# Loading the last two keys of each partition of one K unit by 32 small transfers, in a cached-attention decode layer

## The chip, the cores and the metric

The kernel runs on one core of one Trainium2 chip. The metric is the device time of one execution in microseconds (us), lower is better. Before the change three runs gave 669.81, 669.94 and 670.23 us, a median of 669.94 us. The profile shown here was taken from a separate execution of 670.03 us, of which the span from the first to the last instruction is 668.3 us.

## The reference

One decode step (one new token for each of 4 sequences) of a transformer layer: a layer norm, attention over a cache of 4096 keys and values for each of 32 heads of width 128, an output projection with a residual, then a second layer norm and a small MLP with a Mish activation.

```python
def _A_ref(x, k_cache, v_cache, wq, wo):            # x: 4 x 1 x 640
    q = (x @ wq).reshape(B, Sq, H, Dh).transpose(0, 2, 1, 3)
    scores = jnp.einsum("bhqd,bhkd->bhqk", q, k_cache) * (Dh ** -0.5)
    p = _softmax(scores, axis=-1)
    o = jnp.einsum("bhqk,bhkd->bhqd", p, v_cache)
    return o.transpose(0, 2, 1, 3).reshape(B, Sq, H * Dh) @ wo
...
h = x + _A_ref(_layernorm(x), A_k_cache, A_v_cache, A_wq, A_wo)
h2 = h + _B_ref(_layernorm(h), B_w1, B_b1, B_w2)    # 640 -> 1728 -> 640
```

All tensors are bf16. The K cache and the V cache are 134 MB each (4 x 32 x 4096 x 128 numbers of 2 bytes), the weights some 15 MB together, and everything is read once.

## The kernel before, in words

**Units.** The caches are worked through in 16 units. A unit is 8 heads of one sequence: 8 x 4096 keys, laid on 128 partitions with 16 partitions to a head, so that a partition holds R = 256 consecutive keys of 128 numbers, 64 KB that also lie in one piece in HBM. A unit of K or of V is thus 8.39 MB. The names are `kt0` to `kt15` and `vt0` to `vt15`.

**Slots.** SBUF holds three slots of that size (L71, `bufs=3`), taken in turn: `first` (the query weights `wq` and small inputs), `kt0`, `kt1`, then `vt0` in the place of `first`, `kt2` in that of `kt0`, `vt1` in that of `kt1`, and so on. A load into a slot has to wait until what was there has been read. At the end two slots hold the weights of the projection and the MLP (`wend`, `wend2`).

**Transfers.** All large loads are issued by SyncE, SP for short, in program order: `wq` (L101), then `kt0` and `kt1` (L104 and L105, through `load_kv`, whose `dma_start` is L89), then `vt0` (L239), and in the main loop `kt(u+2)` (L373) and `vt(u+1)` (L378). Two small inputs, `x` (L100, 4 partitions) and `b1` (L102, 1 partition), are issued by ScalarE (ACT). SP is a single sequence: what is queued behind a waiting instruction waits as well. The transfers themselves run on 16 DMA engines.

**Landing signals.** Nobody writes semaphores by hand: the framework gives each transfer one of eight semaphores, in turn over all transfers in program order, ACT's and SP's alike. A reader waits on the semaphore of the transfer it needs. When a transfer gets a semaphore that an earlier one has had, its issue waits until that earlier one has landed. In the program's list of instructions the eight are called DMAHW0 to DMAHW7.

**Compute.** For each unit `scores(u)` multiplies the keys in place by the broadcast query on VectorE (DVE, L263, eight multiplications of 64 keys by 64 columns), sums them with matmuls against the identity (PE, L270) and reductions (DVE, L251). `softmax(u)` (L286 on) takes the maximum and the exponentials (ACT, L309). `pv(u-1)` multiplies with the values of the unit before (PE, L325), and `close` divides by the sums. After the loop come the projection and the MLP.

Of the kernel before, what the change touches and what calls it, by code (L numbers as in the profile page):

```python
# [16 lines left out]
def kernel(  # L17
# [13 lines left out]
    nc = tc.nc  # L31

    B, Sq, D = A_x.shape
    _, H, Sk, Dh = A_k_cache.shape
    F = B_w1.shape[1]
    N = B * Sq
    DC = D // 128
    G = 8
    PH = 128 // G
    R = Sk // PH  # L40
# [38 lines left out]
    def slot(name):  # L79
        return slots.tile([128, SLOT], BF16, tag="kv", name=name)  # L80

    def load_kv(kind, cache, u, parts=1):
        o, b = divmod(u, N)
        t = slot(f"{kind}{u}")
        tv = t[:, :].rearrange("p (r d) -> p r d", d=Dh)
        view = cache[b, G * o : G * (o + 1)].rearrange("h (p r) d -> (h p) r d", p=PH)
        for i in range(parts):
            r0, r1 = i * R // parts, (i + 1) * R // parts
            nc.sync.dma_start(out=tv[:, r0:r1, :], in_=view[:, r0:r1, :])  # L89
        return tv  # L90


    first = slot("first")
    wq_sb = first[:, 0 : DC * H * Dh].rearrange("p (c n) -> p c n", c=DC)
# [7 lines left out]
    nc.scalar.dma_start(out=b1_row, in_=B_b1.rearrange("(o f) -> o f", o=1))  # L102
    kts, vts = {}, {}
    kts[0] = load_kv("kt", A_k_cache, 0)  # L104
    kts[1] = load_kv("kt", A_k_cache, 1)  # L105


    ident = consts.tile([128, 128], BF16)
# [49 lines left out]
    for src, dst in ((ln1_v, xT), (x_v, xT_res)):  # L158
# [10 lines left out]
        out=own1[:, :], in_=ident[:, :].rearrange("p (i k) -> p i k", i=G), axis=AX.X, op=ALU.add  # L169
    )  # L170
    nc.vector.tensor_scalar(
        out=own[:, :], in0=own1[:, :], scalar1=-1.0, scalar2=1e30, op0=ALU.add, op1=ALU.mult
    )
    nc.vector.tensor_reduce(
        out=sel[:, :, :],
        in_=ident[:, :].rearrange("p (t i r) -> p r i t", t=CT, r=RQ),
# [5 lines left out]
        out=dq_f[:, :], in_=ident[:, :].rearrange("p (q j) -> p q j", j=J), axis=AX.X, op=ALU.add  # L182
# [4 lines left out]
        out=j_f[:, :], in_=ident[:, :].rearrange("p (q j) -> p j q", j=J), axis=AX.X, op=ALU.add  # L187
# [287 lines left out]
    for dst in (h2T, hc):  # L475
        nc.vector.tensor_tensor(
            out=dst,
# [10 lines left out]
    for c in range(FC):  # L488
# [9 lines left out]
        if c == 4:  # L498
# [3 lines left out]
                out=std, in_=v_ps[:, :], func=ACT.Sqrt, bias=eps_t[:, :], scale=1.0  # L502
# [4 lines left out]
    def fcn():  # L507
# [4 lines left out]
        out=h1n,  # L512
# [6 lines left out]
        out=h1s,  # L519
# [8 lines left out]
        out=tb, in0=ta, scalar=2.0, in1=ta, op0=ALU.add, op1=ALU.mult  # L528
# [3 lines left out]
        out=tc_, in0=tb, scalar1=-0.5, scalar2=-1.0, op0=ALU.mult, op1=ALU.add  # L532
# [5 lines left out]
        out=act_t, in0=td, scalar=1.0, in1=h1s, op0=ALU.add, op1=ALU.mult  # L538
# [5 lines left out]
    for i, (w2, c) in enumerate(w2_of):  # L544
        rows = 128 if c < C2 else FREM
# [10 lines left out]
        out=oT.rearrange("p n c -> p c n"), in0=hT, in1=y2T[:, :, :], op=ALU.add  # L556
# [43 lines left out]
```

## Time and profile before

| what | value |
|---|---|
| median of 3 runs | 669.94 us (669.81 to 670.23) |
| the profiled execution | 670.03 us, span 668.3 us |
| moved from HBM | 283.35 MB, 424 GB/s over the span |
| time of SP's packets, share of 16 DMA engines | 98.7% |
| PE busy | 383.0 us (57%) |
| DVE busy | 353.2 us (53%) |
| ACT busy | 86.8 us (13%) |

The page gives each engine's busy time and its share of the span; the span in 40 slices of 16.7 us with the busy tenths of each engine, and the rate of the DMA engines; the DMA queues; the chain of work that ended last; the costliest groups of instructions; and the DMA issues. The trace behind it can be asked for the instructions of a line or a tile, for waits, and for the DMA share in any stretch of time. A DMA share of 1.00 means that the 16 engines were busy all the time (packets are counted where they start, so a short stretch can show more than 1). SPq and ACTq are the instructions with which SP and ACT issue transfers. "Landing" is the moment at which a transfer's semaphore says that it is complete.

### The profile page before, as it was taken

To read this page: it belongs to the slowest core of one execution; us is meant where nothing else is said; L and a number is where in the kernel's file an instruction comes from. 1 tells how busy PE (TensorE), PEld (TensorE's weight loads), DVE (VectorE), ACT (ScalarE), POOL (GpSimd) and SP (SyncE) were. 2 spreads that over 40 slices of the span, in tenths; PEclk is the share of its full clock that TensorE was granted. 3 is DMA by queue.
4 is the path that set the end of the run, shared out by engine and by line. 5 is a ranking of instruction groups with operands and counts; after the bars stand their busy time and mean duration, and the time that the engine had idled before them with its cause. 6 is when DMAs were issued, how large, how long until landed. Compare 5 with 4: busy or idle time off the path is not lost.

```text
span 668.3 us, 6430 instructions
## 1 busy us (share of the span) xinstructions
PE 383.0 (57%) x2793; PEld 179.8 (27%) x2793; DVE 353.2 (53%) x314; ACT 86.8 (13%) x314; POOL 1.4 (0%) x10
## 2 busy tenths in 40 slices
PE   0366758375572738557283765738285573728754
PEld 0222323132231313223031322313132231313343
DVE  2078848183663818366381935738192664818321
ACT  0102020202011020202002020110202011020211
POOL 0000000000000000000000000000000000000000
PEclk9998979679696968969698886979888696977965
DMA  9999999999999999999999999999999999999996
GB/s 377 440 439 432 439 433 432 436 428 429 428 436 435 429 432 432 432 436 432 432 432 437 436 421 435 432 436 432 432 428 432 435 432 439 432 440 399 423 415 208
DMA packets 8293, 283.78 MB, mean 425 GB/s; under 512 B 771, under 2 KB 2503, under 8 KB 3144
## 3 DMA queue, kind: packets, MB, share of 16 engines
q1 hardware_dynamic: 8254, 283.35, 98.7%
q8 instruction: 22, 0.36, 0.2%
q14 instruction: 7, 0.06, 0.0%
q10 hardware_dynamic: 10, 0.01, 0.0%
HBM read 283.35 MB, written 0.01 MB: 424 GB/s over the span
## 4 chain that ended last, share of the span: by engine, by line
DMA 59%; DVE 25%; PE 12%; issue 2%; SPq 0%; DVEq 0%; ACT 0%
DMA kt<-in_A_k_cache_dram 55%; DVE kt L263 21%; PE s L270 6%; DMA wend<-in_B_w_dram 5%; PE o L325 4%; DVE s_sb L251 3%; DVE pm L289 1%; PE tr L291 0%; PE tr L302 0%; DVE mx L295 0%; PE h_ps L491 0%; PE y2T L547 0%; SPq L388 0%; DVE otn L354 0%; DVE rl L353 0%
## 5 line engine op out<-in xcount | busy, mean ns | idle before, releaser
L270 PE MATMUL s<-kt,ident 128*128 128x512 bf16 x1024 | 269.7, 418 | 223.6 <-DVE kt L263 223.6
L263 DVE TENSOR_TENSOR kt<-kt,qb 128x4096 bf16<-128x4096 bf16 x128 | 288.1, 2283 | 191.1 <-DMA kt<-in_A_k_cache_dram 191.1
L270 PEld LDWEIGHTS <-ident 128*128 128x128 bf16 x1024 | 108.6, 106 | 378.3 <-issue 148.4
L309 ACT ACTIVATE e<-s_sb,nb 128x256 bf16<-128x256 f32 x128 | 63.1, 494 | 219.0 <-DVE nb L304 219.0
L251 DVE TENSOR_REDUCE s_sb<-s 128x64 f32<-128x512 f32 x64 | 43.9, 687 | 54.6 <-PE s L270 32.6
L325 PE MATMUL o<-vt,e 128*32 128x512 bf16 x1024 | 66.2, 416 | 4.4 <-DMA vt<-in_A_v_cache_dram 4.4
L237 ACT CAST qb<-qb_ps 128x128 bf16<-128x128 f32 x16 | 4.2, 265 | 306.4 <-PE qb_ps L229 306.4
L325 PEld LDWEIGHTS <-e 128*32 128x32 bf16 x1024 | 28.1, 104 | 34.4 <-issue 13.7
L309 ACT ACTIVATION_READ_ACCUMULATOR e<-s_sb,nb 128x1 f32 x128 | 23.8, 186 | 0.0
L291 PE MATMUL tr<-ident_f,pm 128*1 128x128 f32 x32 | 6.1, 270 | 21.3 <-DVE pm L289 21.3
L344 PE MATMUL oT<-sel,o_sb 128*128 128x8 f32 x128 | 17.5, 263 | 1.1 <-ACT o_sb L333 1.1
L344 PEld LDWEIGHTS oT<-sel,o_sb 128*128 128x128 f32 x128 | 16.4, 201 | 1.3 <-ACT o_sb L333 1.3
L353 DVE RECIPROCAL rl<-oT 128x8 f32<-128x8 f32 x16 | 3.2, 199 | 17.0 <-PE oT L344 17.0
L333 ACT COPY o_sb<-o 128x512 f32<-128x512 f32 x16 | 9.1, 569 | 14.7 <-PE o L325 14.7
L202 PE MATMUL qT_ps<-xT,first 128*128 128x4 bf16 x160 | 4.4, 167 | 10.0 <-DMA first<-in_A_wq_dram 10.0
L302 PE MATMUL tr<-mx,nscale 1*128 1x8 f32 x32 | 6.1, 262 | 5.9 <-DVE mx L295 5.9
L291 PEld LDWEIGHTS tr<-ident_f,pm 128*1 128x1 f32 x32 | 1.8, 80 | 28.7 <-issue 28.7
L295 DVE TENSOR_REDUCE mx<-tr 1x8 f32<-1x128 f32 x16 | 4.5, 279 | 9.0 <-PE tr L291 9.0
L302 PEld LDWEIGHTS tr<-mx,nscale 1*128 1x128 f32 x32 | 4.7, 183 | 10.6 <-DVE mx L295 10.6
L216 DVE COPY b1T<-b_ps 128x13 f32<-128x13 f32 x1 | 0.2, 173 | 13.4 <-PE b_ps L213 13.4
L202 PEld LDWEIGHTS <-first 128*128 128x128 bf16 x160 | 4.3, 104 | 10.1 <-DMA first<-in_A_wq_dram 10.1
L340 PEld LDWEIGHTS oT<-rs,ones_f 128*128 128x128 f32 x32 | 6.1, 198 | 3.3 <-issue 1.3
(77 smaller groups left out, 71.8 us busy)
## 6 DMA issues: line engine op xcount, KB each, us to landing
vt<-in_A_v_cache_dram SPq DMA_DIRECT2D x4, 2048.0 KB, 44.0
first<-in_A_wq_dram SPq DMA_DIRECT2D x1, 5120.0 KB, 15.5
wend<-in_A_wo_dram SPq DMA_DIRECT2D x4, 1280.0 KB, 21.3
wend<-in_B_w_dram SPq DMA_DIRECT2D x1, 2160.0 KB
wend<-in_B_w_dram SPq DMA_DIRECT2D x3, 640.0 KB, 17.8
kt<-in_A_k_cache_dram SPq DMA_DIRECT2D x16, 47.9
vt<-in_A_v_cache_dram SPq DMA_DIRECT2D x15, 35.2
wend<-in_B_w_dram SPq DMA_DIRECT2D x1, 160.0 KB, 28.2
```

Source lines behind the costliest of these rows:

```text
L202: nc.tensor.matmul(qT_ps[:, h, :], lhsT=wq_sb[:, c, h * Dh : (h + 1) * Dh], rhs=xT[:, c, :], start=(c == 0), stop=(c == DC - 1),)
L251: nc.vector.tensor_reduce(out=s_sbs[u][:, part * RP : (part + 1) * RP], in_=s_ps[:, :, :], axis=AX.X, op=ALU.add,)
L263: nc.vector.tensor_tensor(out=kt[:, :, d0 : d0 + DQ], in0=kt[:, :, d0 : d0 + DQ], in1=qbs[u][:, d0 : d0 + DQ].unsqueeze(1).to_broadcast([1 ...
L270: nc.tensor.matmul(s_ps[:, :, :], lhsT=ident[:, :], rhs=kt[:, :, d : d + W], start=(d == 0), stop=(d == Dh - W),)
L289: nc.vector.tensor_reduce(out=pm[:, :], in_=s_sb[:, :], axis=AX.X, op=ALU.max)
L291: nc.tensor.matmul(tr_ps[0:1, 0:128], lhsT=pm[:, :], rhs=ident_f[:, :], start=True, stop=True)
L302: nc.tensor.matmul(nb_ps, lhsT=nscale[:, :], rhs=mx[:, :], start=True, stop=True)
L309: nc.scalar.activation(out=e2[:, :, i, :], in_=s_sb[:, :].rearrange("p (g r) -> p g r", r=RQ), func=ACT.Exp, bias=nb[:, i : i + 1], scale= ...
L325: nc.tensor.matmul(o_ps[t : t + G * RQ, :], lhsT=e2[:, g, :, :], rhs=vt[:, g * RQ : (g + 1) * RQ, :], start=(g < CT), stop=(g >= NGV - CT),)
L333: nc.scalar.copy(out=o_sb[:, :], in_=o_ps[:, :])
L340: nc.tensor.matmul(oT_ps[:, 1, :], lhsT=ones_f[:, :], rhs=rss.pop(u)[:, :], start=True, stop=True)
L344: nc.tensor.matmul(oT_ps[:, 0, :], lhsT=o_sb[:, r * Dh : (r + 1) * Dh], rhs=sel[:, r, :], start=(r == 0), stop=(r == RQ - 1),)
```

## The change

`kt1` is loaded by a new helper. One transfer brings the first 254 keys of all 128 partitions. The last two keys of each partition (512 bytes a partition, 64 KB in all) come by 32 transfers: 8 of 8 partitions (partitions 0 to 63), 8 of 4 partitions (64 to 95) and 16 of 2 partitions (96 to 127). All are issued by SP between the load of `kt0` and that of `vt0`. The data and all later work are the same.

```diff
+    def load_k_uneven(u, tail=2):
+
+        o, b = divmod(u, N)
+        t = slot(f"kt{u}")
+        tv = t[:, :].rearrange("p (r d) -> p r d", d=Dh)
+        view = A_k_cache[b, G * o : G * (o + 1)].rearrange("h (p r) d -> (h p) r d", p=PH)
+        nc.sync.dma_start(out=tv[:, 0 : R - tail, :], in_=view[:, 0 : R - tail, :])
+        for rows, lo, hi in ((8, 0, 64), (4, 64, 96), (2, 96, 128)):
+            for p in range(lo, hi, rows):
+                nc.sync.dma_start(
+                    out=tv[p : p + rows, R - tail : R, :], in_=view[p : p + rows, R - tail : R, :]
+                )
+        return tv
...
     kts[0] = load_kv("kt", A_k_cache, 0)
-    kts[1] = load_kv("kt", A_k_cache, 1)
+    kts[1] = load_k_uneven(1)
```

## The prediction

> **What bounds the kernel now.** I read the page first. The DMA row and the queue row say that the kernel is a stream of bytes:
>
> ```profile
> DMA  9999999999999999999999999999999999999996
> GB/s 377 440 439 432 439 433 432 436 428 429 428 436 435 429 432 432 432 436 432 432 432 437 436 421 435 432 436 432 432 428 432 435 432 439 432 440 399 423 415 208
> ...
> q1 hardware_dynamic: 8254, 283.35, 98.7%
> ```
>
> Every slice but the last is at nine tenths or more, while PE and DVE are busy for 57% and 53%. Then I asked for the DMA share by stretches (columns: stretch, its length, busy time of PE, PEld, DVE, ACT and POOL with counts, clock, DMA share, GB/s):
>
> ```profile
> 0.00:1.60 1.60, 0.00 (x0) 0.00 (x0) 0.21 (x2) 0.02 (x1) 0.94 (x8) 1.00 0.00 0
> ...
> 200.00:400.00 200.00, 114.74 (x739) 51.26 (x727) 107.10 (x85) 27.60 (x105) 0.00 (x0) 0.84 1.00 433
> 400.00:560.00 160.00, 91.45 (x572) 40.77 (x572) 85.68 (x68) 20.00 (x76) 0.00 (x0) 0.83 1.00 433
> ```
>
> From 36 to 560 us the share is 1.00 at 433 GB/s: there is no gap in which a lost microsecond could be made up. A unit of 8.39 MB takes 8.39 MB / 433 GB/s = 19.4 us. Whatever leaves the DMA engines without work is added to the end. The question is thus whether SP still queues `vt0` before `kt1` has gone through.
>
> SP's own timeline up to 60 us (start, duration, instruction) and the landings of `kt0` and `kt1`:
>
> ```profile
> 0.74 0.42 SPq L101 DMA_DIRECT2D first<-in_A_wq_dram  x1
> 1.22 0.89 SPq L89 DMA_DIRECT2D kt<-in_A_k_cache_dram  x2
> 21.30 0.33 SPq L89 DMA_DIRECT2D vt<-in_A_v_cache_dram  x1
> 58.52 0.33 SPq L89 DMA_DIRECT2D kt<-in_A_k_cache_dram  x1
> ```
> ```profile
> DMA to landing us min/median/max: 34.7/44.4/54.1
> ```
>
> `kt1` is the second of the pair, issued at 1.7 us, with the longest time: it lands at 1.7 + 54.1 = 55.8 us. `vt0` was queued at 21.3 us, 34 us ahead of need. That is the cover which the change touches.
>
> **What is added, and what it waits for.** One issue becomes 33. A semaphore that comes round again makes the issue wait, and the waits of SP show it in the tail (who waits, for whom, total us, times, longest):
>
> ```profile
> SPq L399 <- DMA wend<-in_A_wo_dram: 1.1, 1, 1.1
> ```
>
> L399 loads `w2` into a slot of its own; nothing in it needs `wo` (L388). It waits for `wo` only because it is given the same semaphore.
>
> Counted in program order: `x` has semaphore 0, `wq` 1, `b1` 2, `kt0` 3, the large part of `kt1` 4. The small transfers go on from there. Numbers 1 to 3 take 5, 6 and 7, which are fresh. Number 4 takes 0 again and waits for `x`, number 5 for `wq`, number 6 for `b1` (early), number 7 for `kt0`, and **number 8 takes semaphore 4 and waits for the large part of `kt1`**. The list of the changed program's instructions has these waits, DMAHW3 on the seventh and DMAHW4 on the eighth. Behind number 8 in SP's single sequence stand numbers 9 to 32 and then `vt0`. At 55.8 us nothing else is queued: the DMA engines run dry, and SP still has 25 small issues (8 to 32) to make before `vt0`.
>
> **Price of one small issue.** The trace of before has no issue of 8, 4 or 2 partitions on SP. Nearest rows by place: the four issues of `wo` take 1.75 us together, the two of `kt` 0.89 us, so 0.44 to 0.47 us each with the gap between them. These four at 624.4 us include one whose semaphore had come round and was free. By size, ACT's two small issues bound it:
>
> ```profile
> 0.73 0.55 ACTq L100 DMA_DIRECT2D first<-in_A_x_dram  x1
> 1.31 0.23 ACTq L102 DMA_DIRECT2D first<-in_B_b_dram  x1
> ```
>
> Four partitions took 0.55 us (0.58 to the next start), one partition 0.23 us, 0.27 with a gap of 0.04; SP's store of 20 partitions (L568) took 0.39. I take 0.47 us, SP's own spacing, which lies between, and keep 0.27 and 0.58 for the range. 25 x 0.47 = 11.8 us (6.8 to 14.5).
>
> That holds if a small transfer lands before its semaphore comes round eight issues later, 8 x 0.47 = 3.8 us. The store at the end is issued at 666.1 us and everything is over at 668.3; `x`, issued at 0.73 us, let DVE start at 3.19. Both are under 2.5 us, so the spacing decides and not the landing.
>
> **Sum.** `vt0` is issued at 55.8 + 11.8 = 67.6 us instead of 21.3. What does the stream lose? Restarting costs what it costs at the launch. Up to the end of `kt1` the engines move 5.24 (`wq`) + 8.39 + 8.39 = 22.02 MB, at 433 GB/s 50.9 us, after a start-up S counted from the span's beginning; so on the mean they finish at 50.9 + S. Restarted, they are as good as at full rate S - 0.74 after the issue (the issue of `wq` was at 0.74 us). The loss is 67.6 + (S - 0.74) - (50.9 + S) = 16.0 us, in which S cancels. The large part is 2 of 256 keys shorter: 0.15 us off, 15.8.
>
> That is the mean of 16 engines. With S = 2.2 us (the first slice moved 377 instead of 433 GB/s for 16.7 us: 2.2 us lost) they finish at 53.1 us, while the last landing is at 55.8: some engines run late. If an engine that is late here is also the one that ends the kernel, it loses less, for the pause lets it catch up: at most the 2 us or so between the two times, which gives 13.8. No view names the engines, so I keep both and take 15.5, nearer to the mean.
>
> In a sentence apart: the Trainium skill ("DMA: Bandwidth & Descriptors", section "Latency and other measured facts") gives about 600 ns to the first byte of a transfer issued by SP; here the first packets start between 1.60 and 1.80 us, some 1.0 us after the issue at 0.74. By the page's figure the sum would be 0.4 us lower, 15.1; the measurement decides.
>
> **What costs nothing.** The 64 KB themselves move while the engines are idle anyway. The multiplications of `kt1` start at 61.06 us as before, since only those of the last 64 keys need the small pieces; they come some 16 us later, and the last piece should land by 69 or 70. So `kt1` is used up as before and `vt1` is issued at 84.7 as before. `vt0` lands at 75.1 + 15.5 = 90.6 instead of 75.1 (21.3 + 53.8 in its row); the matmuls of `pv(0)`, at 87.1 before, wait until then, and `kt3`, queued behind them, is issued 3.5 us later, at 94.3, while `kt2` is still moving (88.5 to 110). No second gap, and after that everything is shifted alike.
>
> 670.03 + 15.5 = 685.5 us in the profiled execution; the median of before lies 0.09 us under it, so **685.4 us**.
>
> **Rivals.**
> 1. *Hidden: not slower.* If number 8 didn't have to wait for `kt1`, SP would go on from `kt0`'s landing (1.2 + 34.7 = 35.9 us), issue 26 pieces by 48.1 us and `vt0` right then, ahead of the 53 us at which the engines get free. That is the point from which it decides: `vt0` queued before 52. What is left is the pieces' own time: between -0.15 us (an engine relieved of its share of them) and +2.4 us (all 64 KB on one engine at 433 / 16 = 27 GB/s); with the pieces spread unevenly over some engines about +0.5, so 670.4 us. For it: `vt0` has 34 us of cover. Against it: the wait on DMAHW4 is in the program, and L399's row shows that such waits hold. Chance 0.05, within no change mostly.
>    The Trainium skill (same page, section "Issuing engines are not separate DMA queues") says that the sequencer's time to start a transfer is usually small relative to the transfer. By that rule this rival would win. The rows agree for a unit (0.47 against 19.4 us), but not for a piece of 1 to 4 KB, which needs less than 0.2 us.
> 2. *Landing-bound.* If small pieces land slowly, each semaphore comes round only after its landing, and the spacing is landing time / 8. From 3.8 us on that replaces 0.47; at 5 us it is 0.62 and gives 25 x 0.62 + 3.7 = 19.2, so 689 us. For it: nothing but the unknown size. Against it: the landings under 2.5 us. Chance 0.07.
> 3. *Cheap issues.* Pieces of one to eight rows cost like L102: 0.27 us, sum 6.8 + 3.7 = 10.5 us, 680.4 us (678.8 if the late engines decide). Chance 0.23.
> 4. *Given back later*: 560 to 625 us has a share of 0.98, so about 1.3 us at most could be absorbed: 684.1 us, inside the forecast's own range.
>
> **How the numbers follow.** The forecast, a stall of the stream at `kt1` with an issue of 0.4 to 0.58 us, has 0.65: 682 to 688.5 us. Rival 3 has 0.23, rival 2 0.07, rival 1 0.05. The range goes from 678.8 (rival 3 with late engines) to 689.0; it leaves out rival 1 and the far parts of rival 2. 0.2% is 1.3 us, about what a measurement of this kernel can tell from no change: faster 0.01, same 0.04 (rival 1 mostly), slower 0.95.
>
> **What would show it.** In SP's timeline: small issues 1 to 4 by 4 us, 5 and 6 at 16, number 7 near 36, then nothing until 55.6, then 25 issues some 0.47 apart and `vt0` at 67 to 68. In the stretches: a DMA share near zero from 56 to 68, and 1.00 again after 70. In PE's row: `pv(0)` waiting for `vt` to about 90.6. The chain at the end (from 624 us on) the same, 15.5 us later. I am wrong if `vt0` is issued before 55 us; if the spacing of the small issues is far from 0.47; or if the gap is there and the end doesn't move by as much.

## The result and the profile after

The changed kernel takes 681.59 us (median of 4 runs, 681.39 to 681.67) against 669.88 us before on the same chip: ratio 1.0173, 95% interval 1.0161 to 1.0185, 11.71 us slower. The profiled execution has a span of 679.9 us, 11.6 more than before.

The page's DMA rows show where it went. They are the same rows as before the change, in 40 slices of 17.0 us:

```profile
DMA  9993999999999999999999999999999999999996
GB/s 375 448 448 151 432 426 436 425 432 432 433 429 432 433 428 432 429 432 429 437 432 441 432 440 429 432 429 436 429 432 429 436 429 432 429 436 417 421 416 204
...
q1 hardware_dynamic: 8510, 283.35, 97.1%
```

One slice, the fourth (51 to 68 us), falls to 3 tenths and 151 GB/s; the others are close to what they were. The same 283.35 MB are moved. The stretches (columns as in the prediction, the last two are DMA share and GB/s) give the edges of the hole:

```profile
53.00:56.00 3.00, 2.69 (x13) 1.13 (x12) 3.00 (x3) 0.00 (x0) 0.00 (x0) 1.00 0.07 15
56.00:62.00 6.00, 3.39 (x17) 1.28 (x15) 3.21 (x4) 0.00 (x0) 0.00 (x0) 1.00 0.02 5
62.00:66.00 4.00, 1.54 (x6) 0.71 (x7) 3.74 (x3) 3.54 (x15) 0.00 (x0) 0.81 0.79 264
...
70.00:100.00 30.00, 15.41 (x117) 6.50 (x115) 14.41 (x12) 4.97 (x19) 0.00 (x0) 0.92 1.00 433
...
400.00:560.00 160.00, 94.39 (x608) 42.38 (x611) 87.26 (x72) 21.12 (x81) 0.00 (x0) 0.85 1.00 433
```

From 53 to 62 us hardly any packets but those of the small pieces start; from 70 us on the share is 1.00 at 433 GB/s again, and nothing is made up later. SP's timeline has the reason (start, duration, instruction):

```profile
1.65 0.45 SPq L98 DMA_DIRECT2D kt<-in_A_k_cache_dram  x1
2.15 61.02 SPq L101 DMA_DIRECT2D kt<-in_A_k_cache_dram  x32
63.29 0.36 SPq L89 DMA_DIRECT2D vt<-in_A_v_cache_dram  x1
63.76 0.36 SPq L89 DMA_DIRECT2D kt<-in_A_k_cache_dram  x1
```

`vt0` (the third line) is issued at 63.29 us instead of 21.30. In front of it stand the 32 small issues, merged into one row of 61 us because they wait in between. What SP waited for (us in total, times, longest):

```profile
SPq L101 <- DMA kt<-in_A_k_cache_dram: 38.3, 2, 19.4
...
SPq L101 <- DMA first<-in_A_wq_dram: 12.5, 1, 12.5
```

Two waits for K units of 38.3 us together: number 7 for `kt0`, number 8 for `kt1`. The other row is number 5, which stood for `wq`. Asked from 55 to 64 us alone, the timeline shows the part that falls into the hole:

```profile
55.45 7.72 SPq L101 DMA_DIRECT2D kt<-in_A_k_cache_dram  x25
```

Just 25 issues, from 55.45 us, the landing of the large part of `kt1`. The spacing is (63.29 - 55.45) / 25 = 0.31 us.

### The profile page after: what moved, and what is told of

It reads as the page before. It is cut to its first block, busy times and chain, and to the rows that moved or that the text cites. A ratio compares the mean times of both kernels' runs of the same rounds, so it can differ in the third digit from the quotient of the medians.

```text
span 679.9 us, 6471 instructions
## 1 busy us (share of the span) xinstructions
PE 383.8 (56%) x2793; PEld 180.1 (26%) x2793; DVE 353.3 (52%) x314; ACT 87.0 (13%) x314; POOL 1.4 (0%) x10
## 3 DMA queue, kind: packets, MB, share of 16 engines
q1 hardware_dynamic: 8510, 283.35, 97.1%
HBM read 283.35 MB, written 0.01 MB: 417 GB/s over the span
## 4 chain that ended last, share of the span: by engine, by line
DMA 58%; DVE 23%; PE 10%; another core or an unknown queue 5%; issue 2%; SPq 1%; DVEq 0%; ACT 0%
DMA kt<-in_A_k_cache_dram 53%; DVE kt L277 18%; DMA wend<-in_B_w_dram 5%; PE s L284 5%; PE o L339 4%; DVE s_sb L265 3%; SPq L101 1%; DVE pm L303 0%; PE tr L305 0%; PE tr L316 0%; PE h_ps L505 0%; PE y2T L561 0%; DVE mx L309 0%; SPq L402 0%
## 5 line engine op out<-in xcount | busy, mean ns | idle before, releaser
L265 DVE TENSOR_REDUCE s_sb<-s 128x64 f32<-128x512 f32 x64 | 44.0, 688 | 54.1 <-PE s L284 33.6
L339 PE MATMUL o<-vt,e 128*32 128x512 bf16 x1024 | 67.8, 423 | 5.9 <-DMA vt<-in_A_v_cache_dram 5.9
L305 PE MATMUL tr<-ident_f,pm 128*1 128x128 f32 x32 | 6.1, 270 | 21.3 <-DVE pm L303 21.3
L303 DVE TENSOR_REDUCE pm<-s_sb 128x1 f32<-128x256 f32 x16 | 6.7, 420 | 0.5
```

The costliest lines, as they stand in the source:

```text
L265: nc.vector.tensor_reduce(out=s_sbs[u][:, part * RP : (part + 1) * RP], in_=s_ps[:, :, :], axis=AX.X, op=ALU.add,)
L303: nc.vector.tensor_reduce(out=pm[:, :], in_=s_sb[:, :], axis=AX.X, op=ALU.max)
L305: nc.tensor.matmul(tr_ps[0:1, 0:128], lhsT=pm[:, :], rhs=ident_f[:, :], start=True, stop=True)
L339: nc.tensor.matmul(o_ps[t : t + G * RQ, :], lhsT=e2[:, g, :, :], rhs=vt[:, g * RQ : (g + 1) * RQ, :], start=(g < CT), stop=(g >= NGV - CT),)
```

## The experiments

The theory under test: SP must see a large transfer land before it can queue the next one, because a small issue in front of it has that transfer's semaphore; the stream then stands still for that wait, for each small issue that is left, and for the restart. In one rule, the loss is the time at which the next unit is queued, less 0.74 us (the first issue of the launch), less the megabytes up to there at 433 GB/s. Rival A puts the loss on the pieces' own transfer, which falls on few engines. Rival B puts it on SP's issue time as such, without a semaphore.

**Seven and six pieces.** The helper's loop is replaced by fewer transfers, so that only the last place moves (each kernel has one of the two lines with a `+` and a `for`; the comments say which):

```diff
-        for rows, lo, hi in ((8, 0, 64), (4, 64, 96), (2, 96, 128)):
-            for p in range(lo, hi, rows):
...
+        for lo, hi in ((0, 64), (64, 96), (96, 112), (112, 120), (120, 124), (124, 126), (126, 128)):   # seven
+        for lo, hi in ((0, 64), (64, 96), (96, 112), (112, 120), (120, 124), (124, 128)):               # six
+            nc.sync.dma_start(out=tv[lo:hi, R - tail : R, :], in_=view[lo:hi, R - tail : R, :])
```

> The last two keys come by 7 transfers (64, 32, 16, 8, 4, 2 and 2 partitions) instead of 32; vt0 is now the one that gets the semaphore of the large part of kt1. Theory (the stream runs dry because SP must see kt1 land before it can queue vt0, and then pays for each issue that still stands before it): vt0 is issued at 55.5 us with no small issue left in front, the loss is 55.5 - 0.74 - 50.9 = 3.9 us, so 673.8 us. Rival A (the loss of 11.7 us is the pieces' own transfer time on few engines): 64 KB in fewer, more even pieces, so less than a quarter of it, 670 to 672.5 us, and no gap in the DMA share. Rival B (SP's issue time as such, 32 x 0.31 us and no semaphore in it): 7 x 0.4 = 2.8 us, 672.7 us, or nothing.

> As with seven transfers, but six (64, 32, 16, 8, 4 and 4 partitions), so that vt0 gets the semaphore of kt0, which lands at 36 us. Theory: vt0 is issued near 36.3 us, 17 us before the engines get free, no gap, 669.9 us as before the change (within 0.5). Rival A and rival B see no difference between six and seven transfers: both within 0.4 us of the kernel with seven.

Seven took 673.68 us, six 670.10; before, in the same session, 669.82. The ratio of six to before is 1.0004 (0.9995 to 1.0013), no difference; that of seven is 1.0056 (1.0040 to 1.0073). The issue of `vt0` in SP's timeline, of seven and then of six:

```profile
55.76 0.36 SPq L89 DMA_DIRECT2D vt<-in_A_v_cache_dram  x1
```
```profile
36.34 0.36 SPq L89 DMA_DIRECT2D vt<-in_A_v_cache_dram  x1
```

and the DMA share from 53 to 57 us, of seven and then of six:

```profile
53.00:57.00 4.00, 2.79 (x13) 1.07 (x11) 3.96 (x3) 0.00 (x0) 0.00 (x0) 1.00 0.68 213
```
```profile
53.00:57.00 4.00, 3.53 (x16) 1.43 (x15) 4.00 (x3) 0.00 (x0) 0.00 (x0) 1.00 1.23 496
```

The bytes are the same, and splitting 4 partitions into 2 and 2 costs 3.6 us. With six, `vt0` itself has `kt0`'s semaphore and is queued at 36.34 us, with cover to spare. With seven it has `kt1`'s and is queued when `kt1` has landed. Neither A nor B has a step between six and seven. The rule gives 55.76 - 0.74 - 50.9 = 4.1 us for seven, measured 3.9: that is the price of the wait and the restart with no small issue behind it.

**Sixty-four pieces.** All pieces of 2 partitions, in place of the change's loop:

```diff
+        for p in range(0, 128, 2):
+            nc.sync.dma_start(out=tv[p : p + 2, R - tail : R, :], in_=view[p : p + 2, R - tail : R, :])
```

> The same 64 KB by 64 transfers of 2 partitions. Theory: transfers 8 to 64 stand behind the landing of kt1, 57 x 0.296 = 16.9 us, vt0 issued at 72.4 us, loss 72.4 - 0.74 - 50.9 = 20.8 us, so 690.7 us. Rival A (transfer time on the most loaded engines: 64 pieces on each of two engines instead of 32): double of 11.7 us, 693.3 us. Rival C (the loss is the landing wait and a restart, and the number of issues matters little): 682 us.

690.72 us, ratio 1.0312 (1.0296 to 1.0327), 20.9 us slower; the theory had 690.7, rival A 693.3, rival C 682. `vt0` in SP's timeline, and the durations of the small issues between 60 and 73 us (ns minimum, median, maximum):

```profile
72.80 0.36 SPq L89 DMA_DIRECT2D vt<-in_A_v_cache_dram  x1
```
```profile
L100 SPq DMA_DIRECT2D kt<-in_A_k_cache_dram x43: 251/252/253, 60.0 to 72.4; - x43
```

The slope is as steep as SP's spacing: 32 issues more cost 690.72 - 681.59 = 9.1 us, 0.29 us each.

**The 32 pieces by GpSimd.** The same transfers, issued by GpSimd (POOL) behind its constants, in a helper called after L119's `memset`. Against the change this line differs:

```diff
-                nc.sync.dma_start(
+                nc.gpsimd.dma_start(
                     out=tv[p : p + rows, R - tail : R, :], in_=view[p : p + rows, R - tail : R, :]
```

> The very 32 transfers of the change, but issued by GpSimd, which is idle after its few constants and has eight semaphores of its own, so that nothing of SP waits for them before vt1 at 84.7 us. Theory: vt0 is queued at 21.3 us, no gap, 669.9 us (up to 670.8 if the pieces' own time shows). Rival A: the pieces are the same and the loss stays, 680 to 682 us. Rival B: SP is relieved, 670 us as by the theory; the six and the seven transfers tell these two apart.

686.06 us, ratio 1.0242 (1.0227 to 1.0258). The expectation of 669.9 to 670.8 was wrong, and the number even exceeds rival A's. But the hole isn't at 53 us any more. `vt0` is queued at 21.3 us and the share stays at 1.02 from 56 to 62 us; it is zero here:

```profile
94.00:107.00 13.00, 6.42 (x16) 2.22 (x16) 5.41 (x4) 0.00 (x0) 2.05 (x4) 0.54 0.01 0
```

The next rows are DVE's (with the idle time before it and what ended that), SP's issue of `vt1`, and POOL's transfers of 2 partitions on the page (KB each, median us to landing):

```profile
97.88 2.29 DVE L281 TENSOR_TENSOR kt<-kt,qb 128x4096 bf16<-128x4096 bf16 x1 [19.61 <-DMA kt<-in_A_k_cache_dram]
```
```profile
106.68 0.33 SPq L89 DMA_DIRECT2D vt<-in_A_v_cache_dram  x1
```
```profile
kt<-in_A_k_cache_dram POOLq DMA_DIRECT2D x16, 1.0 KB, 21.0
```

The 21 us are a median of 16 pieces of 1 KB that went out at different times. Their landings, of the five issued between 40 and 60 us beside the full stream, and then of the last four, issued from 94.6 us on, when the stream was dry:

```profile
DMA to landing us min/median/max: 33.6/34.8/36.2
```
```profile
DMA to landing us min/median/max: 1.6/1.6/1.6
```

A piece of 1 KB needs some 34 us when it shares the DMA engines with the full stream. POOL's eight semaphores came round, it waited for landings 21 times, and the last piece was issued near 96 us. The last 64 keys of `kt1` waited 19.6 us for it, `kt1`'s slot came free late, and `vt1` was queued at 106.68 instead of 84.73. Up to there 22.02 + 2 x 8.39 = 38.8 MB have to move, 89.6 us at 433 GB/s: 106.68 - 0.74 - 89.6 = 16.3 us by the same rule, measured 16.2. My expectation overlooked that the pieces are slow beside a full stream, and that `kt1`'s slot is the cover that they use up. The mechanism stands: a unit was queued too late. But the run doesn't isolate the semaphore, as it was meant to, since another wait came in its place; that the semaphore is the cause rests on the six and the seven pieces.

The Trainium skill ("DMA: Bandwidth & Descriptors", section "Issuing engines are not separate DMA queues") says that transfers from SP, ACT and GpSimd all run on the same 16 engines and interleave. This run fits that: the pieces that GpSimd issued beside SP's stream took 33.6 to 36.2 us to land, those without it 1.6.

**Pieces of all partitions.** One key of 128 partitions a piece, so the large part has 224 keys. (A piece has 32 KB, all of them 1.05 MB. The text below says 64 KB and four keys a piece, which is wrong; its 16 times the bytes is right.)

```diff
-    def load_k_uneven(u, tail=2):
+    def load_k_uneven(u, tail=32):
...
+        for r in range(R - tail, R):
+            nc.sync.dma_start(out=tv[:, r : r + 1, :], in_=view[:, r : r + 1, :])
```

> 32 transfers again, but each of one key of all 128 partitions (so the last 32 keys come apart, and the large part has 224 keys and lands near 53.1 us). It separates what one issue costs from how many partitions it has. If SP's spacing grows with the partitions, as the prediction's 0.47 us for the 128-partition issues of before has it: vt0 at 53.1 + 25 x 0.47 = 64.9 us, loss 64.9 - 0.74 - 50.9 = 13.3, 683.1 us. If every issue costs the 0.31 us of the small ones and 0.47 was due to a busy queue: vt0 at 61.0 us, loss 9.4, 679.3 us. If the pieces' transfer time counted, 64 KB a piece of four keys and 16 times the bytes in all would give far more than 13 us.

683.39 us, ratio 1.0202 (1.0185 to 1.0219), 13.5 us slower; 683.1 was the branch in which the price grows with the partitions. Durations of these issues in ns from 54 to 70 us, and their landing:

```profile
L100 SPq DMA_DIRECT2D kt<-in_A_k_cache_dram x24: 429/430/432, 53.6 to 64.5; - x24
```
```profile
DMA to landing us min/median/max: 1.7/2.0/2.5
```

An issue of 128 partitions takes 0.43 us (spaced 0.47) also when the engines have little else to do. That of 2 partitions takes 0.25. The bytes hardly count: the issue of `kt0` in this kernel, 8.39 MB over 128 partitions, took 0.41 us. And with 16 times the bytes in the pieces the loss is 1.8 us larger than that of the change, by as much as `vt0` is queued later (65.07 against 63.29 us); rival A has no room here.

**The pieces behind `vt0`.** The 32 transfers of the change on SP, moved behind L239's load of `vt0`:

```diff
     vts[0] = load_kv("vt", A_v_cache, 0)
+    pieces()
```

> The 32 transfers of the change, on SP, but issued after vt0 instead of before it. vt0 is queued at 21.3 us as before the change. Theory: number 8 now gets the semaphore of vt0 and waits for its landing at 75.1 us; 25 issues of 0.31 us follow, kt2 is queued at 83.1 instead of 58.5 us, when the stream has been dry for as long: loss 83.1 - 0.74 - (22.02 + 8.39 MB) / 433 GB/s = 83.1 - 0.74 - 70.2 = 12.1 us, 681.9 us, with the gap at 73 to 84 us instead of 53 to 64. Rival (the stall is a matter of the launch, or of standing in front of vt0; with vt0 queued early it is hidden): 670 us.

681.44 us, ratio 1.0172 (1.0157 to 1.0187), 11.5 us slower: the same loss as the change. `vt0` is queued at 21.02 us here, yet:

```profile
21.39 61.11 SPq L103 DMA_DIRECT2D kt<-in_A_k_cache_dram  x32
82.62 0.36 SPq L89 DMA_DIRECT2D kt<-in_A_k_cache_dram  x1
```
```profile
72.00:75.00 3.00, 1.87 (x8) 0.78 (x8) 3.00 (x2) 0.00 (x0) 0.00 (x0) 1.00 0.04 10
```

Now `kt2` is the unit that comes late, at 82.62 us instead of 58.52, and the share is 0.04 from 72 to 75 us. The hole has moved by one unit and kept its size. By the rule 82.62 - 0.74 - 70.2 = 11.7 us.

All of them in one table, "queued" being the issue of the late unit:

| kernel | late unit | queued, us | MB up to there | loss by the rule | loss measured |
|---|---|---|---|---|---|
| the change | `vt0` | 63.29 | 22.02 | 11.7 | 11.7 |
| seven pieces | `vt0` | 55.76 | 22.02 | 4.1 | 3.9 |
| sixty-four pieces | `vt0` | 72.80 | 22.02 | 21.2 | 20.9 |
| by GpSimd | `vt1` | 106.68 | 38.80 | 16.3 | 16.2 |
| pieces of 128 partitions | `vt0` | 65.07 | 22.02 | 13.4 | 13.5 |
| behind `vt0` | `kt2` | 82.62 | 30.41 | 11.7 | 11.5 |

One rule holds for losses from 3.9 to 20.9 us at three places, within 0.3 us. It takes the queued time from each trace, so the table tests how a late unit turns into lost time; what made the unit late is shown by the waits and by six against seven.

## Why the prediction was right, and which term was mis-sized

- *The wait* was right: number 8 stood until `kt1` had landed (forecast 55.6 us, measured 55.45), numbers 1 to 4 were issued by 4 us, 5 and 6 at 16, 7 at 36.2. Six against seven pieces shows that it is the semaphore. A mere limit of eight transfers under way would give the same step, but it doesn't fit number 5: DVE was reading `x` from 2.2 us on and all packets of ACT's two transfers had started by 2.5 us, yet number 5 stood until 16.24 us, the landing of `wq`, whose semaphore it has.
- *25 issues behind it, then `vt0`* was right in the count. *Their price* was the term that failed: 0.47 us was taken from SP's issues of 128 partitions. In the hole the one issue of 8 partitions took 0.27 us, those of 4 partitions 0.29 and those of 2 partitions 0.25, with gaps 0.31 on the mean. 25 x 0.47 = 11.8 became 7.84 us, 3.9 us less, and that is the distance from 685.4 to 681.59 but for 0.1 (`kt1` landed 0.2 us earlier than forecast, and 0.3 us allowed for late engines was not needed; the two nearly cancel). The pieces of 128 partitions show that 0.47 was no wrong reading: it is the price of that size. No row of before gave the price of the small ones. Of ACT's two, one partition at 0.23 us lay near and four partitions at 0.55 us far off, and both stood at the launch, where the changed kernel's own first piece of 8 partitions took 0.50 us against 0.27 in the hole. A spacing far from 0.47 was one of the prediction's signs of being wrong, and it came. The time, 681.59, stands nearer to the third rival (cheap issues, 680.4) than to the forecast; it misses the forecast's own 682 to 688.5 by 0.4, and lies within the full range because that was drawn to take in the third rival.
- *The sum of the stream* was right to 0.1 us once the issue time is put in. The allowance for late engines (15.5 instead of 15.8) was not needed at the end: the loss is that of the mean. In between it shows: the first multiplication of `kt15` went from 600.54 to 610.87 us, 10.3 later, while the end moved by 11.6. That engines which had been late caught up in the hole would explain it, but no view names the engines, so it isn't shown.
- *Landing-bound* (second rival) is out: the issues of 2 partitions followed each other at 0.25 us and a constant gap (251, 252 and 253 ns with sixty-four pieces), so none of them waited for a semaphore to come round. Even pieces of 32 KB landed in 1.7 to 2.5 us on empty engines. With eight issues of 0.30 us making 2.4 us the margin was thinner than I thought.
- *Hidden* (first rival) fell with the timeline. The kernel with six pieces is what it described, and it does come out at 670.1. The Trainium skill ("DMA: Bandwidth & Descriptors", section "Issuing engines are not separate DMA queues") had the rule that went with it, that the time to start a transfer is usually small relative to the transfer. The trace agrees for a unit (an issue of 0.33 to 0.43 us against 19.4 us). For a piece of 1 KB the issue took 0.25 us; the transfer's own 0.04 us is an estimate from 433 / 16 = 27 GB/s an engine, and no run shows it by itself.
- *The first byte*: `vt0`'s first packets started at 64.28 us, 1.0 us after the start of its issue at 63.29, as at the launch of before (1.78 after 0.74). Counted from the end of the issue instruction (63.65 and 1.16 us) it is 0.6 us at both places. The Trainium skill ("DMA: Bandwidth & Descriptors", section "Latency and other measured facts") gives about 600 ns. The trace agrees with it by the second count, so the 0.4 us that the prediction saw between page and trace is a matter of where the count starts.
- *What was to be late next* was overstated, since the hole was smaller. `pv(0)` started at 87.2 us, not at 90.6, and `kt3` was issued at 90.87 against 90.77 before. `kt1`'s multiplications began at 62.34 instead of 61.06, which cost nothing.

## What to carry to other kernels

Where a framework gives out a few semaphores in turn, count them from each small transfer back by that number: if it meets a large transfer, the issuing engine stops until that one has landed, and everything queued behind it loses its lead. In a kernel bound by its stream the loss can be worked out before a run: the time at which the next large transfer is queued, less the time at which the engines run out of bytes, plus the restart. Six pieces in front of the next large load cost nothing here; a seventh cost 3.6 us.

## What the runs showed of the hardware that I had not expected

- SP's issues of transfers, one after the other into DMA engines that have little else to do, took 0.25 us for 2 partitions, 0.29 for 4 and 0.43 for 128. It isn't a plain slope: the one of 8 partitions took 0.27. At the launch the prices differ: 0.50 us for the first piece of 8 partitions in the change, 0.92 for the piece of 64 in the kernel with six.
- Pieces of 1 KB that GpSimd issued took 33.6 to 36.2 us to land beside the full stream of 64 KB rows, and 1.6 us once it had run dry. Pieces of 32 KB from SP landed in 1.7 to 2.5 us while the engines had little else to do. The company counts for more than the size.
